# A decayed linear attention and two gated layers on one core: the norm without small instructions, the own term of the first tiles summed by TensorE, and r multiplied as it leaves PSUM

## The chip, the core and the metric

The kernel runs on one core of a Trainium2 chip. The core has five engines with their own instruction queues: TensorE (PE in the profile; its weight loads are listed apart as PEld), VectorE (DVE), ScalarE (ACT), GpSimd (POOL) and SyncE (SP), which here only issues DMA transfers. Matmuls write PSUM, eight banks of 128 partitions by 512 float32. The metric is the time of one execution on the device in microseconds; of several runs the median.

## The reference, cut to what matters

Three things follow each other. First an attention with a decaying state over 4 batches, 8 heads, 768 steps and head size 48:

```python
for t in range(S):
    kt, vt, rt = k[:, :, t], v[:, :, t], r[:, :, t]
    cur = np.einsum('bhd,bhe->bhde', u[None] * kt, vt)
    y[:, :, t] = np.einsum('bhd,bhde->bhe', rt, state + cur)
    state = w[None, :, :, None] * state + np.einsum('bhd,bhe->bhde', kt, vt)
```

Its output, as 3072 tokens of 384 columns, is normalised and goes through two gated layers of width 1536:

```python
rms = np.sqrt(np.mean(x * x, axis=-1, keepdims=True) + 1e-06)
xn = x / rms * rms_g
g = xn @ w_gate                       # layer one: silu(g) * (xn @ w_val) @ w_out
...
gate = 1.0 / (1.0 + np.exp(-(x @ w_gate)))
return (gate * (x @ w_val) @ w_out).astype(np.float32)   # layer two
```

The term with u is what a token contributes to its own output: for each head the sum over d of r, u and k, times v. It is called the own term below. The weights of the two layers come as float64 and are turned into float32 on the chip.

## The kernel before

**Tiles and blocks.** The tokens are cut into 24 tiles of 128 (tile i is chunk i // 4 of batch i % 4, so tiles 0 to 3 are the first chunk of each batch and start without a state), and into 6 blocks of four tiles for the gated layers. A layer takes each block through 12 steps, one for every 128 columns of the width of 1536; a step multiplies x with a piece of w_gate and a piece of w_val (lines 687 to 689: three float32r products each, of the high and low parts of weights and x) and accumulates the product with a piece of w_out (line 714). Layer one's six blocks are followed by layer two's. The 36 pieces of layer one's weights are fetched and converted in the first block's steps (ScalarE lines 66, 71 and 649, VectorE lines 80, 81 and 652, GpSimd line 87).

**A tile of attention** (`attention(i)`, from line 459) works with k divided and r multiplied by powers of w, taken from the middle of the tile. VectorE or GpSimd makes kq = kn * wk and rq = rn * wr (line 474); for tiles 1 to 7 TensorE turns both (line 332) and ScalarE moves them from PSUM into kT and rT (line 498); from tile 8 on the turn goes through DRAM. Tile 0's k and r are turned raw in the set-up and multiplied with the powers tq and tp, which lie in the buffers o[2] and o[1], as they leave PSUM (line 322). TensorE then computes scores and state change (`both`, lines 508 and 513) into two banks; VectorE masks the scores into aa (line 519), and forms zh, the state in the middle of the tile (a copy, line 527, in tiles 0 to 3; a sum with z, line 529, later), and zu (line 532). The result (lines 541 and 548) needs zh and aa, and VectorE adds the own term vc while it takes the result out of PSUM into x (line 554).

**The own term** vc is made by two products, a reduction to cf and a product with vn (lines 474, 483, 474).

**The norm:** ScalarE squares x with a running sum (line 563), VectorE folds a check on that sum into ok (line 565) and turns the sum into the mean plus epsilon (line 568), GpSimd raises it to the power -1/2 (line 473), and VectorE scales x by it and by g (line 572). TensorE turns x (line 583), and ScalarE and VectorE make xh and xl from it (lines 587 and 589), which the steps read.

**Order.** Nothing is ordered by hand. Every instruction, or small group, is added to a plan with a duration estimate per engine, a due time, and the tokens it reads and writes; `Plan.run` then simulates the engines with these estimates and emits each engine's instructions in the order that comes out. A task that names two engines ("VG") goes to the one that the plan finds done first. A changed estimate, or a task less, can therefore change the order of the whole beginning. On the chip each engine runs its list in order and waits where it must.

Of the kernel before, what the change touches and what calls it, by code (L numbers as in the profile page):

```python
# [15 lines left out]
P = 128  # L16
# [214 lines left out]
def blocked(  # L231
# [36 lines left out]
    wsafe = const.tile([HS, NPAIR], F32, name="wsafe")  # L268
    p2 = const.tile([HS, 8, NPAIR], F32, name="p2")
# [9 lines left out]
    totals = const.tile([P, 2 * 3 * NF], F32, name="totals")  # L279
    mhalf = const.tile([P, 1], F32, name="mhalf")  # L280
# [40 lines left out]
    def mul(e, out, x, y, op=ALU.mult):  # L321
        e.tensor_tensor(out=out, in0=x, in1=y, op=op)
# [11 lines left out]
    def setup():  # L334
# [130 lines left out]
    def attention(i):  # L465
# [16 lines left out]
        add("VG", (0.47, 1.02), d + 1, either(vc[i2], vc[i2], u_bc, ALU.mult), (), [("vc", i2)])  # L482
        add("V", 0.46, d + 3, lambda: nc.vector.tensor_reduce(
            out=cf[i2].rearrange("p h o -> p (h o)"), in_=vc[i2], axis=AX.X, op=ALU.add), [("vc", i2)], [("cf", i2)])
        add("VG", (0.47, 0.9), d + 4, either(vc[i2], vn[i3], cf[i2].to_broadcast([P, H, D]), ALU.mult),
            [("v", i3), ("cf", i2)], [("vc", i2)])
# [71 lines left out]
        if not last:  # L558
# [3 lines left out]
        t = ss[i2]  # L562
# [403 lines left out]
```

## Time and profile before

| | us |
|---|---|
| median of 3 runs (1031.54 to 1032.87) | 1032.0 |
| the profiled execution | 1029.34 |
| its span, first to last instruction | 1027.7 |
| TensorE busy in the span | 1002.4 (98%) |
| VectorE | 490.4 (48%) |
| ScalarE | 341.7 (33%) |
| GpSimd | 140.2 (14%) |

The profile is of one execution. Busy times are of the whole span; the kernel has stretches with different limits, so a share of the whole says little about any one of them. TensorE's clock as granted was 0.989 of full in the mean; it is at half in parts of the first 50 us.

### The profile page before, as it was taken

To read this page: it belongs to the slowest core of one execution; us is meant where nothing else is said; L and a number is where in the kernel's file an instruction comes from. 1 tells how busy PE (TensorE), PEld (TensorE's weight loads), DVE (VectorE), ACT (ScalarE), POOL (GpSimd) and SP (SyncE) were. 2 spreads that over 40 slices of the span, in tenths; PEclk is the share of its full clock that TensorE was granted. 3 is DMA by queue.
4 is the path that set the end of the run, shared out by engine and by line. 5 is a ranking of instruction groups with operands and counts; after the bars stand their busy time and mean duration, and the time that the engine had idled before them with its cause. 6 is when DMAs were issued, how large, how long until landed. Compare 5 with 4: busy or idle time off the path is not lost.

```text
span 1027.7 us, 19397 instructions
## 1 busy us (share of the span) xinstructions
PE 1002.4 (98%) x7938; PEld 831.1 (81%) x7938; DVE 490.4 (48%) x993; ACT 341.7 (33%) x710; POOL 140.2 (14%) x170
## 2 busy tenths in 40 slices
PE   7799999999999999999999999999999999999997
PEld 6577777787787777778888888888888888888886
DVE  7889995645655664653555322222222223222222
ACT  3577552223333333334555312222212222112221
POOL 4443432212321320211110000000000000000000
PEclk8899999999999999999999999999999999999998
DMA  8916356555884785653654100100100000000001
GB/s 195 274 41 157 91 110 143 106 104 129 178 175 123 156 189 135 145 148 94 198 171 147 62 1 3 59 1 22 40 1 31 32 1 5 27 1 27 4 1 34
DMA packets 213761, 91.40 MB, mean 89 GB/s; under 512 B 156576, under 2 KB 205984, under 8 KB 213664
## 3 DMA queue, kind: packets, MB, share of 16 engines
q1 hardware_dynamic: 213664, 90.08, 35.3%
q8 instruction: 64, 1.05, 0.5%
q14 instruction: 33, 0.27, 0.1%
HBM read 64.10 MB, written 25.95 MB: 88 GB/s over the span
## 4 chain that ended last, share of the span: by engine, by line
PE 87%; DVE 8%; DMA 1%; ACT 1%; issue 1%; POOL 0%; SPq 0%; DVEq 0%; POOLq 0%; ACTq 0%
PE bank L714 27%; PE bank L687 18%; PE bank L688 18%; PE bank L689 18%; PE bank L548 2%; DVE wraw L81 1%; PE bank L541 1%; PE bank L508 1%; DVE w L652 1%; DVE wt L80 1%; DVE hl L699 1%; DMA rn<-in_r_dram 1%; PE bank L513 1%; DVE vc L474 1%; DVE sg L696 0%
## 5 line engine op out<-in xcount | busy, mean ns | idle before, releaser
L687 PE MATMUL bank<-xh,w 128*128 128x512 f32 x864 | 344.5, 399 | 1.8 <-ACT w L649 1.1
L689 PE MATMUL bank<-xh,w 128*128 128x512 f32 x864 | 342.5, 396 | 0.3 <-DVE w L652 0.3
L688 PE MATMUL bank<-xl,w 128*128 128x512 f32 x864 | 342.6, 397 | 0.0
L696 DVE TENSOR_TENSOR sg<-bank,sg 128x512 f32<-128x512 f32 x144 | 99.2, 689 | 371.5 <-PE bank L689 368.2
L689 PEld LDWEIGHTS bank<-xh,w 128*128 128x128 f32 x864 | 162.7, 188 | 40.7 <-DVE w L652 2.3
L687 PEld LDWEIGHTS bank<-xh,w 128*128 128x128 f32 x864 | 162.8, 188 | 39.2 <-ACT w L649 2.4
L688 PEld LDWEIGHTS bank<-xl,w 128*128 128x128 f32 x864 | 162.8, 188 | 35.4 <-DVE xl L589 0.3
L694 ACT ACTIVATE sg<-bank 128x512 f32<-128x512 f32 x144 | 85.9, 597 | 294.0 <-PE bank L689 293.9
L698 ACT ACTIVATE hh<-sg 128x512 fp32r<-128x512 f32 x144 | 90.7, 630 | 238.5 <-DVE sg L696 238.5
L714 PE MATMUL bank<-w,hh 128*128 128x384 f32 x576 | 158.7, 337 | 0.0
L714 PE MATMUL bank<-hh,w 128*128 128x512 f32 x432 | 151.3, 401 | 0.7 <-DVE w L652 0.7
L699 DVE TENSOR_TENSOR hl<-sg,hh 128x512 fp32r<-128x512 f32 x144 | 102.2, 710 | 65.3 <-ACT hh L698 65.0
L714 PEld LDWEIGHTS bank<-w,hh 128*128 128x128 f32 x576 | 105.0, 188 | 3.4
L714 PEld LDWEIGHTS bank<-hh,w 128*128 128x128 f32 x432 | 81.0, 188 | 21.2 <-DVE w L652 1.6
L714 PE MATMUL bank<-w,hl 128*128 128x384 f32 x288 | 96.7, 336 | 0.0
L714 PE MATMUL bank<-hl,w 128*128 128x512 f32 x216 | 85.4, 395 | 0.0
L87 POOL TENSOR_TENSOR wt<-wraw 128x384 int32<-128x384 int32 x36 | 33.1, 918 | 200.1 <-DVE wraw L81 118.8
L66 ACT ACTIVATE wt<-wraw 128x384 f32<-128x384 f32 x72 | 39.7, 552 | 51.5 <-DMA wraw<-in_moe_w_gate_dram 23.0
L714 PEld LDWEIGHTS bank<-w,hl 128*128 128x128 f32 x288 | 54.1, 188 | 3.3 <-DVE hl L699 0.3
L714 PEld LDWEIGHTS bank<-hl,w 128*128 128x128 f32 x216 | 40.6, 188 | 8.7
L87 POOL TENSOR_TENSOR wraw<-wraw 128x384 int32<-128x384 int32 x36 | 37.8, 1060 | 54.4 <-DVE wraw L81 31.4
L81 DVE SCALAR_TENSOR_TENSOR wraw<-wraw,wt 128x384 int32<-128x384 int32 x72 | 41.8, 589 | 1.4
(122 smaller groups left out, 712.6 us busy)
## 6 DMA issues: line engine op xcount, KB each, us to landing
wraw<-in_moe_w_gate_dram SPq DMA_DIRECT2D x24, 384.0 KB, 4.4
wraw<-in_moe_w_val_dram SPq DMA_DIRECT2D x24, 384.0 KB, 4.5
wraw<-in_moe_w_out_dram SPq DMA_DIRECT2D x24, 384.0 KB, 5.0
parked<-wt SPq DMA_DIRECT2D x36, 192.0 KB, 2.7
wt<-parked SPq DMA_DIRECT2D x36, 192.0 KB, 2.4
kn<-in_k_dram SPq DMA_DIRECT2D x24, 192.0 KB, 3.7
rn<-in_r_dram SPq DMA_DIRECT2D x24, 192.0 KB, 4.1
vn<-in_v_dram SPq DMA_DIRECT2D x24, 192.0 KB, 3.8
```

The costliest lines, as they stand in the source:

```text
L66: nc.scalar.activation(t.bitcast(F32), raw[:, :, 1].bitcast(F32), AF.Abs, scale=2.0 ** -112, accum_out=total)
L81: yield nc.vector.scalar_tensor_tensor(out=high, in0=high, scalar=-(1 << 31), in1=t, op0=ALU.bitwise_and, op1=ALU.bitwise_or)
L87: nc.gpsimd.tensor_tensor(out=out, in0=raw[:, :, 1], in1=raw[:, :, 0], op=ALU.add)
L548: nc.tensor.matmul(yp[n][part(s)][ts, p * D:(p + 1) * D], aa[0][part(s), n, p, ts], vn[i3][part(s), 2 * p + n, :], start=(first and not s ...
L687: nc.tensor.matmul(ps, whi[f][:, kind, ws], xh[b2][:, c, :], start=(c == 0), stop=False)
L688: nc.tensor.matmul(ps, whi[f][:, kind, ws], xl[b2][:, c, :], start=False, stop=False)
L689: nc.tensor.matmul(ps, wlo[f][:, kind, ws], xh[b2][:, c, :], start=False, stop=(c == KC - 1))
L694: add("A", 0.6, d - STEP, lambda g: nc.scalar.activation(sg[n2], g, gate), [("g", n)], [("sg", n2)], psum=[("g", n)])
L696: add("V", 0.69, d + 1 - STEP, lambda ps: nc.vector.tensor_tensor(out=sg[n2], in0=ps, in1=sg[n2], op=ALU.mult), [("value", n)], [("sg", n2 ...
L698: add("A", 0.63, d + 1 - STEP, lambda: nc.scalar.activation(hh[n2], sg[n2], AF.Copy), [("sg", n2)], [("hh", n2)])
L699: add("VG", (0.69, 1.5), d + 1 - STEP, lambda e: by[e].tensor_tensor(out=hl[n2], in0=sg[n2], in1=hh[n2].bitcast(F32), op=ALU.subtract), [( ...
L714: nc.tensor.matmul(a[:, :rhs.shape[-1]], lhsT, rhs, start=(f == 0 and i == 0), stop=(f == NF - 1 and i == 2))
```

## The change

Three edits. In the **norm**, x and vc become views of buffers that are one column wider (x_ and vc_); that column of x_ holds the square root of EPS * 384, so the scaled sum of squares over 385 columns is the mean plus epsilon at once. The steps at lines 565 and 568 are gone; the sums of all tiles stay in `squares` and are checked with three instructions in `weights_ok`, late in layer one. GpSimd's power reads the sum itself.

For tiles 0 to 3 the **own term** is made otherwise: VectorE multiplies kT by rT (in which the powers of w cancel but for one factor w), TensorE multiplies that product with uw = u * w, one column per pair of heads and half tile, into the last four columns of the two banks of scores, and VectorE multiplies vn with these columns as they leave PSUM, a half tile at a time. uw is loaded by two more transfers in the set-up.

In tiles 1 to 7 **r** is turned raw, and VectorE multiplies it with the powers while it moves it from PSUM into rT; the product rq on VectorE or GpSimd and ScalarE's move are gone. In tiles 0 to 3 ScalarE, not VectorE, copies zh.

```diff
+    uw = const.tile([HS, NPAIR], F32, name="uw")
+    squares = const.tile([P, NTILE], F32, name="squares")
...
+    x_, vc_ = ring("x", 2, [P, DM + 1]), ring("vc", 2, [P, DM + 1])
+    x, vc = [t[:, :DM] for t in x_], [t[:, :DM].rearrange("p (h d) -> p h d", h=H) for t in vc_]
...
         load_heads(kn[0], k, 0, 0)
         load_heads(rn[0], r, 0, 0)
+        for n in range(2):
+            nc.sync.dma_start(out=uw[rows(n)], in_=u.rearrange("(p a) d -> a d p", a=2)[n])
...
+        for t in x_:
+            nc.gpsimd.memset(t[:, DM:], (EPS * DM) ** 0.5)
...
+    def own_factors():
+        mul(nc.vector, uw, uw, wsafe)
...
-        if i:
+        if by_dma:
             add("VG", (0.47, 1.02), d - 2, either(rq_, rn_, heads(wr), ALU.mult), [("r", i2)], ["rq"])
-        add("VG", (0.47, 1.02), d + 1, either(vc[i2], rn_, kn_, ALU.mult), [("r", i2), ("k", i2)], [("vc", i2)])
...
+        by_sums = i < B
+        if not by_sums:
+            add("VG", (0.47, 1.02), d + 1, either(vc[i2], rn_, kn_, ALU.mult), [("r", i2), ("k", i2)], [("vc", i2)])
...
-            for nm, src, read, dst in (("kT", kq[i2], ("kq", i2), kT[i2]), ("rT", rq[0], "rq", rT[i2])):
+            for nm, src, read, dst in (("kT", kq[i2], ("kq", i2), kT[i2]), ("rT", rn[i2], ("r", i2), rT[i2])):
...
-                add("A", 0.48, d + (nm == "rT"), lambda ps, dst=dst: nc.scalar.activation(dst[:HS], pairs(ps), AF.Copy),
-                    [name(nm)], tokens, psum=[name(nm)])
+                if nm == "kT":
+                    add("A", 0.48, d, lambda ps, dst=dst: nc.scalar.activation(dst[:HS], pairs(ps), AF.Copy),
+                        [name(nm)], tokens, psum=[name(nm)])
+                else:
+                    add("V", 0.6, d + 1, lambda ps, dst=dst: nc.vector.tensor_tensor(out=dst[:HS], in0=pairs(ps), in1=pairs(o[1]), op=ALU.mult),
+                        [name(nm), ("o", 1)], tokens, psum=[name(nm)])
...
+        if by_sums:
+            prod, token = ((o[0], ("o", 0)), (sg[0], ("sg", 0)))[i2]
+            add("V", 0.6, d + 3, lambda: nc.vector.tensor_tensor(out=pairs(prod), in0=kT[i2], in1=rT[i2][:HS], op=ALU.mult),
+                [(t, i2, n) for t in ("kT", "rT") for n in range(2)], [token], port=True)
+            own = lambda sp: sp[:, N - NPAIR:]
+
+            def sums(*sp):
+                for p in range(NPAIR):
+                    for s in range(2):
+                        for n in range(2):
+                            nc.tensor.matmul(own(sp[n])[part(s), p:p + 1], pairs(prod)[rows(n), p, part(s)], uw[rows(n), p:p + 1],
+                                             start=True, stop=True)
+            add("T", 0.5, d + 4, sums, [token, "uw", name("sp")], [name("own")], psum=banks)
+            for n in range(2):
+                add("V", 0.27, d + 5, lambda sp, n=n: nc.vector.tensor_tensor(
+                    out=half_of(vc[i2], n), in0=half_of(vn[i3], n), in1=own(sp).unsqueeze(2).to_broadcast([P, NPAIR, D]), op=ALU.mult),
+                    [name("own"), ("v", i3)], [("vc", i2)], psum=[banks[n]])
...
-            add("V", 0.27, d + 4, lambda sp: nc.vector.tensor_copy(zh[i2], u3(sp)), [name("sp")], [("zh", i2)], psum=banks[:1])
+            add("A", 0.27, d + 4, lambda sp: nc.scalar.activation(zh[i2], u3(sp), AF.Copy), [name("sp")], [("zh", i2)], psum=banks[:1])
...
-        add("A", 0.5, d + 7, lambda: nc.scalar.activation(flat(vc[i2]), x[i2], AF.Square, accum_out=t[:, 0:1]),
-            [("x", i2)], [("vc", i2), ("ss", i2)])
-        add("V", 0.07, d + 20, lambda: nc.vector.scalar_tensor_tensor(
-            out=ok, in0=t[:, 0:1], scalar=3e38, in1=ok, op0=ALU.is_le, op1=ALU.mult), [("ss", i2)], ["ok"])
-        t_ = small[i2]
-        add("V", 0.07, d + 8, lambda: nc.vector.tensor_scalar(
-            out=t_[:, 0:1], in0=t[:, 0:1], scalar1=1.0 / DM, scalar2=EPS, op0=ALU.mult, op1=ALU.add),
-            [("ss", i2)], [("rms", i2)])
-        add("G", 0.55, d + 8, tt(nc.gpsimd, t_[:, 1:2], t_[:, 0:1], mhalf, ALU.pow), (), [("rms", i2)])
+        mean, t_ = squares[:, i:i + 1], small[i2]
+        add("A", 0.5, d + 7, lambda: nc.scalar.activation(vc_[i2], x_[i2], AF.Square, scale=DM ** -0.5, accum_out=mean),
+            [("x", i2)], [("vc", i2), ("square", i)])
+        add("G", 0.55, d + 8, tt(nc.gpsimd, t_, mean, mhalf, ALU.pow), [("square", i)], [("rms", i2)])
...
+        nc.vector.tensor_scalar(out=squares, in0=squares, scalar1=3e38 / DM, scalar2=None, op0=ALU.is_le)
+        nc.vector.tensor_reduce(out=one, in_=squares, axis=AX.X, op=ALU.min)
+        mul(nc.vector, ok, ok, one)
...
+    plan.add("V", 0.1, DUE[0][0], own_factors, (), ["uw"])
```

The plan puts out another order. On VectorE, the list right after the set-up's last product (into rT of tile 0) before; the number behind a name marks one buffer, so that rT_115 is tile 0's and rn_96 and kn_98 are tile 1's:

```order
L322 TENSOR_TENSOR rT_115<-bank_76,o_139 112x512
L474 TENSOR_TENSOR vc_105<-rn_95,kn_97 128x384
L474 TENSOR_TENSOR kq_103<-kn_98,wk 128x8x48
L474 TENSOR_TENSOR vc_105<-vc_105,u_bc 128x384
L474 TENSOR_TENSOR rq_104<-rn_96,wr 128x8x48
L483 TENSOR_REDUCE cf_107<-vc_105 128x8
L519 TENSOR_TENSOR aa_117<-bank_73,mask 128x4x64
L519 TENSOR_TENSOR aa_117<-bank_74,mask 128x4x64
L474 TENSOR_TENSOR vc_105<-vn_99,cf_107 128x384
L527 COPY zh_124<-bank_73 112x192
```

and now, with o_139 the powers for r and o_138 the product of kT and rT of tile 0:

```order
L327 TENSOR_TENSOR rT_113<-bank_76,o_139 112x512
L327 TENSOR_TENSOR uw<-uw,wsafe 112x4
L547 TENSOR_TENSOR o_138<-kT_111,rT_113 112x512
L487 TENSOR_TENSOR kq_105<-kn_100,wk 128x8x48
L519 TENSOR_TENSOR rT_114<-bank_73,o_139 112x512
L327 TENSOR_TENSOR sg_133<-sg_133 112x4 x3
L327 TENSOR_TENSOR p_84<-sg_133 112x4
L438 COPY wc<-p_84 112x192
L540 TENSOR_TENSOR aa_115<-bank_74,mask 128x4x64
L540 TENSOR_TENSOR aa_115<-bank_75,mask 128x4x64
L559 TENSOR_TENSOR vc_118<-vn_101,bank_74 128x4x48
L571 TENSOR_TENSOR zu_126<-bank_75,zh_124 112x192
```

The two products into vc, the reduction and the copy of zh are gone from between set-up and tile 0's own part; uw, the product of kT and rT, and tile 1's rT stand there, and the state factors wc have moved ahead of aa.

On TensorE, the instructions at the start of the first step (xh_128 with w), before; vn_100 is tile 4's v, and x_119 tile 3's x:

```order
L548 MATMUL bank_78<-vn_100,aa_117 32x48 x4
L548 MATMUL bank_77<-vn_100,aa_117 32x48 x4
L583 MATMUL bank_75<-ident,x_119 128x128 x3
L687 MATMUL bank_73<-xh_128,w_803 128x512
L688 MATMUL bank_73<-xl_130,w_803 128x512
L689 MATMUL bank_73<-xh_128,w_803 128x512
```

and now, where vn_101 is tile 3's v, rn_97 tile 4's r, x_116 tile 2's x and x_117 tile 3's:

```order
L587 MATMUL bank_73<-vn_101,aa_115 32x48 x4
L587 MATMUL bank_79<-vn_101,aa_115 32x48 x4
L337 MATMUL bank_80<-ident,rn_97 112x128 x4
L616 MATMUL bank_76<-ident,x_116 128x128 x3
L616 MATMUL bank_77<-ident,x_117 128x128 x3
L720 MATMUL bank_74<-xh_128,w_804 128x512
L721 MATMUL bank_74<-xl_130,w_804 128x512
```

The scores and the result of tile 4 stood ahead of the first step; now only the turn of its r does, with the turns of x of tiles 2 and 3.

On ScalarE, around the first two xh (line 587), before:

```order
L587 ACTIVATE xh_128<-bank_79 128x3x128
L563 ACTIVATE vc_106,ss_110<-x_119 128x384
L66 ACTIVATE wt_146,totals<-wraw_313 128x384
L71 ACTIVATE wraw_313<-wraw_313 128x384
L498 ACTIVATE kT_114<-bank_75 112x512
L498 ACTIVATE rT_116<-bank_73 112x512
L587 ACTIVATE xh_128<-bank_74 128x3x128
```

and now, where L620 is the step into xh and L566 the copy zh of tiles 2 and 3:

```order
L602 ACTIVATE vc_119,squares<-x_117 128x385
L620 ACTIVATE xh_128<-bank_73 128x3x128
L566 ACTIVATE zh_124<-bank_78 112x192
L66 ACTIVATE wt_146,totals<-wraw_320 128x384
L71 ACTIVATE wraw_320<-wraw_320 128x384
L620 ACTIVATE xh_128<-bank_77 128x3x128
L566 ACTIVATE zh_125<-bank_75 112x192
L602 ACTIVATE vc_118,squares<-x_116 128x385
```

Each of the two copies zh stands right behind a step into xh that belongs to the tile two before it.

## Rows read from the trace of the kernel before

**Rows 1.** Stretches: busy us of PE, PEld, DVE, ACT, POOL; granted clock; DMA share, GB/s:
```profile
11.20:46.10 34.90, 25.13 (x780) 20.70 (x780) 29.79 (x82) 15.71 (x41) 14.96 (x15) 0.80 1.01 253
46.10:141.00 94.90, 90.38 (x828) 69.02 (x829) 90.26 (x181) 64.91 (x164) 40.02 (x40) 0.98 0.43 112
141.00:1028.00 887.00, 879.02 (x6291) 734.10 (x6290) 363.43 (x685) 257.56 (x496) 80.68 (x91) 1.00 0.32 79
12.00:18.00 6.00, 4.85 (x110) 4.13 (x105) 5.60 (x16) 2.58 (x7) 2.80 (x2) 0.50 1.14 278
```

**Rows 2.** TensorE's waits, longest first, 11.2 to 46.1: total us, times, longest:
```profile
PE bank L541 <- DVE zh L527: 2.6, 2, 1.4
...
```

**Rows 3.** TensorE's longest wait, 46.1 to 141 us:
```profile
PE bank L687 <- ACT w L649: 1.1, 2, 0.8
```

**Rows 4.** VectorE's groups, 11.2 to 141 us: busy us, mean ns | idle before, releaser:
```profile
...
L699 DVE TENSOR_TENSOR hl<-sg,hh 128x512 fp32r<-128x512 f32 x11 | 8.8, 799 | 1.0 <-ACT hh L698 0.9
...
L554 DVE TENSOR_TENSOR x<-bank,vc 128x192 f32<-128x192 f32 x16 | 5.5, 348 | 1.7 <-PE bank L548 1.6
L474 DVE TENSOR_TENSOR vc<-rn,kn 128x384 f32<-128x384 f32 x8 | 5.0, 625 | 0.0
L474 DVE TENSOR_TENSOR vc<-vc,u_bc 128x384 f32<-128x384 f32 x8 | 4.4, 547 | 0.0
L483 DVE TENSOR_REDUCE cf<-vc 128x8 f32<-128x384 f32 x8 | 4.3, 540 | 0.0
L474 DVE TENSOR_TENSOR vc<-vn,cf 128x384 f32<-128x384 f32 x6 | 4.3, 712 | 0.0
L565 DVE SCALAR_TENSOR_TENSOR ok<-ss,ok 128x1 f32<-128x1 f32 x8 | 3.9, 494 | 0.0
L474 DVE TENSOR_TENSOR rq<-rn,wr 128x384 f32<-128x384 f32 x6 | 3.9, 648 | 0.1
L589 DVE TENSOR_TENSOR xl<-bank,xh 128x384 fp32r<-128x384 f32 x7 | 3.9, 554 | 2.4 <-ACT xh L587 2.4
L474 DVE TENSOR_TENSOR kq<-kn,wk 128x384 f32<-128x384 f32 x6 | 3.3, 549 | 0.7 <-DMA kn<-in_k_dram 0.7
...
L474 DVE TENSOR_TENSOR z<-zu,wc 112x192 f32<-112x192 f32 x5 | 1.7, 346 | 0.0
L527 DVE COPY zh<-bank 112x192 f32<-112x192 f32 x4 | 1.4, 348 | 0.0
...
L568 DVE TENSOR_SCALAR rms<-ss 128x1 f32<-128x1 f32 x8 | 1.2, 145 | 0.0
L322 DVE TENSOR_TENSOR rT<-bank,o 112x512 f32<-112x512 f32 x1 | 0.7, 681 | 0.0
```

**Rows 5.** Timeline 36.2 to 38.5 us: start, duration, engine, instruction:
```profile
36.28 0.15 DVE L565 SCALAR_TENSOR_TENSOR ok<-ss,ok 128x1 f32<-128x1 f32 x1
36.35 0.35 DVE L80 TENSOR_SCALAR wt<-wt 128x384 int32<-128x384 int32 x1
...
37.59 0.83 POOL L87 TENSOR_TENSOR wraw<-wraw 128x384 int32<-128x384 int32 x1 [3.63 <-DVE rms L568]
...
37.75 0.68 DVE L565 SCALAR_TENSOR_TENSOR ok<-ss,ok 128x1 f32<-128x1 f32 x1
```

**Rows 6.** TensorE's timeline, tile five (from 88 us) and tile zero (13.57):
```profile
13.57 0.89 PE L513 MATMUL bank<-vn,kq 64*48 64x48 f32 x32 [1.15 <-POOL kq L474]
...
88.50 0.60 PE L332 MATMUL bank<-ident,kq 128*112 128x128 f32 x4
...
92.33 0.71 PE L508 MATMUL bank<-rT,kT 48*64 48x64 f32 x32 [0.69 <-ACT rT L498]
92.84 0.55 PE L513 MATMUL bank<-vn,kq 64*48 64x48 f32 x32
...
98.37 0.32 PE L541 MATMUL bank<-z,rT 48*64 48x48 f32 x4
...
99.12 0.89 PE L548 MATMUL bank<-vn,aa 64*32 64x48 f32 x64
```

More of the change, by code (lines that the diff above doesn't have):

```diff
@@ L279, in blocked @@
     totals = const.tile([P, 2 * 3 * NF], F32, name="totals")
+    squares = const.tile([P, NTILE], F32, name="squares")
     mhalf = const.tile([P, 1], F32, name="mhalf")
     rn, kn, vn = ring("rn", 2, [P, H, PAD]), ring("kn", 2, [P, H, PAD]), ring("vn", 3, [P, H, D])
-    kq, rq, vc = ring("kq", 2, [P, H, PAD]), ring("rq", 1, [P, H, PAD]), ring("vc", 2, [P, H, D])
-    cf, ss, small = ring("cf", 2, [P, H, 1]), ring("ss", 2, [P, 1]), ring("rms", 2, [P, 2])
+    kq, rq = ring("kq", 2, [P, H, PAD]), ring("rq", 1, [P, H, PAD])
+    cf, small = ring("cf", 2, [P, H, 1]), ring("rms", 2, [P, 1])
     kT, rT, aa = ring("kT", 2, [HS, NPAIR, P]), ring("rT", 2, [P, NPAIR, P]), ring("aa", 1, [P, 2, NPAIR, P])
-    x, z = ring("x", 2, [P, DM]), ring("z", B, [HS, NPAIR, D])
+    x_, vc_ = ring("x", 2, [P, DM + 1]), ring("vc", 2, [P, DM + 1])
+    x, vc = [t[:, :DM] for t in x_], [t[:, :DM].rearrange("p (h d) -> p h d", h=H) for t in vc_]
+    z = ring("z", B, [HS, NPAIR, D])
     zh, zu = ring("zh", 2, [HS, NPAIR, D]), ring("zu", 2, [HS, NPAIR, D])
@@ L347, in setup @@
             nc.sync.dma_start(out=wT[rows(n)], in_=w.rearrange("(p a) d -> a d p", a=2)[n])
-        for t in (kn[0], rn[0], kq[1], rq[0]):
+        nc.gpsimd.memset(uw, 1.0)
+        for t in (kn[0], rn[0], kq[1], rn[1], rq[0]):
             nc.gpsimd.memset(t[:, :, D:], 0.0)
@@ L477, in attention @@
         add("VG", (0.47, 1.02), d - 2, either(kq_, kn_, heads(wk), ALU.mult), [("k", i2)], [("kq", i2)])
-        if i:
+        if by_dma:
             add("VG", (0.47, 1.02), d - 2, either(rq_, rn_, heads(wr), ALU.mult), [("r", i2)], ["rq"])
-        add("VG", (0.47, 1.02), d + 1, either(vc[i2], rn_, kn_, ALU.mult), [("r", i2), ("k", i2)], [("vc", i2)])
[L482 to L486, printed above, removed]
+        by_sums = i < B
+        if not by_sums:
+            add("VG", (0.47, 1.02), d + 1, either(vc[i2], rn_, kn_, ALU.mult), [("r", i2), ("k", i2)], [("vc", i2)])
+            add("VG", (0.47, 1.02), d + 1, either(vc[i2], vc[i2], u_bc, ALU.mult), (), [("vc", i2)])
+            add("V", 0.46, d + 3, lambda: nc.vector.tensor_reduce(
+                out=cf[i2].rearrange("p h o -> p (h o)"), in_=vc[i2], axis=AX.X, op=ALU.add), [("vc", i2)], [("cf", i2)])
+            add("VG", (0.47, 0.9), d + 4, either(vc[i2], vn[i3], cf[i2].to_broadcast([P, H, D]), ALU.mult),
+                [("v", i3), ("cf", i2)], [("vc", i2)])
         if by_dma:
@@ L559, in attention @@
             add("VG", (0.27, 0.6), d + 10, either(z[b], zu[i2], wc, ALU.mult), ["wc", ("zu", i2)], [("z", b)])
-        t = ss[i2]
-        add("A", 0.5, d + 7, lambda: nc.scalar.activation(flat(vc[i2]), x[i2], AF.Square, accum_out=t[:, 0:1]),
-            [("x", i2)], [("vc", i2), ("ss", i2)])
-        add("V", 0.07, d + 20, lambda: nc.vector.scalar_tensor_tensor(
-            out=ok, in0=t[:, 0:1], scalar=3e38, in1=ok, op0=ALU.is_le, op1=ALU.mult), [("ss", i2)], ["ok"])
-        t_ = small[i2]
-        add("V", 0.07, d + 8, lambda: nc.vector.tensor_scalar(
-            out=t_[:, 0:1], in0=t[:, 0:1], scalar1=1.0 / DM, scalar2=EPS, op0=ALU.mult, op1=ALU.add),
-            [("ss", i2)], [("rms", i2)])
-        add("G", 0.55, d + 8, tt(nc.gpsimd, t_[:, 1:2], t_[:, 0:1], mhalf, ALU.pow), (), [("rms", i2)])
+        mean, t_ = squares[:, i:i + 1], small[i2]
+        add("A", 0.5, d + 7, lambda: nc.scalar.activation(vc_[i2], x_[i2], AF.Square, scale=DM ** -0.5, accum_out=mean),
+            [("x", i2)], [("vc", i2), ("square", i)])
+        add("G", 0.55, d + 8, tt(nc.gpsimd, t_, mean, mhalf, ALU.pow), [("square", i)], [("rms", i2)])
         add("V", 0.53, d + 9, lambda: nc.vector.scalar_tensor_tensor(
-            out=x[i2], in0=x[i2], scalar=t_[:, 1:2], in1=g_bc, op0=ALU.mult, op1=ALU.mult), [("rms", i2)], [("x", i2)], port=True)
+            out=x[i2], in0=x[i2], scalar=t_, in1=g_bc, op0=ALU.mult, op1=ALU.mult), [("rms", i2)], [("x", i2)], port=True)
         to = (slice(None), slice(None), slice(col * P, (col + 1) * P))
@@ L793, in blocked @@
         if (bi, f) == (turn - 1, NF - 1):
-            plan.add("V", 0.6, at[turn, 3], weights_ok, [("total", i) for i in range(2 * 3 * NF)], ["ok"])
+            plan.add("V", 0.6, at[turn, 3], weights_ok, [("total", i) for i in range(2 * 3 * NF)] + [("square", i) for i in range(NTILE)], ["ok"])
             plan.add("T", 0.1, at[turn, 3], count_bad, ["ok"], ["count"], psum=["count"])
```

## The prediction

> **What bounds the kernel now.** I read the table of stretches first, cut where the work changes character: the set-up of the powers of w (to 11.2 us), the first four tiles of attention (to 46.1, where TensorE begins the first GLU step), the stretch until tile seven's x stands ready in xh and xl (141.0), and the rest [rows 1]. In the rest TensorE is busy 879.0 of 887.0 us, and the list of waits names none for TensorE there; the 8 us that are left are the tail behind its last matmul. Nothing on another engine can shorten that stretch. All that can be won lies in the first 141 us.
>
> In 11.2 to 46.1 TensorE is busy 25.1 of 34.9 us and VectorE 29.8; in 46.1 to 141.0 both are busy 90.3 or 90.4 of 94.9, so neither has room [rows 1]. TensorE's longest wait in the first of the two is for zh, a copy on VectorE, 2.6 us in two waits; in the second the longest are for a piece of weights, 1.1 us in two [rows 3]. I take VectorE as the bound of both stretches: it runs its list almost without a gap, and TensorE's gaps end when VectorE gets to the next item. The DMA share of 1.01 in the first stretch [rows 1] is the other candidate; against it speaks that VectorE waited for a transfer only 0.7 us there, for kn [rows 4], because most of the traffic is weights fetched far ahead.
>
> **The change, part by part.** I count VectorE's instructions in the order of both kernels from the end of set-up to the eighth subtraction into xl (tile seven's). Both have the same 35 pieces of weights and the same GLU instructions in between, so the stretches compare, and the mean durations of the stretch 11.2 to 141 price the rest [rows 4].
>
> What goes, 41 instructions: 8 of ok at 0.494 us (3.95), 8 of rms at 0.145 (1.16), 4 reductions into cf at 0.540 (2.16), 5 products into rq at 0.648 (3.24; six were there and one, tile eight's, stays), of the products into vc 3 of rn by kn at 0.625 (1.88), 4 by u_bc at 0.547 (2.19) and 2 of vn by cf at 0.712 (1.42), 3 of z at 0.346 that the planner now gives to GpSimd (1.04), and 4 copies zh at 0.348 that go to ScalarE (1.39). Sum 18.4 us.
>
> What comes, 22 instructions: 7 products of a transposed r in PSUM with the powers, 112x512, for which the set-up's own rT is the same instruction, 0.681 (4.77); 4 products of kT by rT, 112x512 out of SBUF, which the trace does not have: between 0.549 (kq, 384 wide) and 0.799 (hl, 512 wide), and I take 0.681 (2.72); 8 half-width products of vn with the own term out of PSUM, like the sums into x, 0.348 (2.78); 2 more of kq, which GpSimd had, 0.549 (1.10); one product uw, 0.15. Sum 11.5 us.
>
> The difference is 6.9 us of durations. Neighbours overlap: an ok lasts 0.15 us and the next instruction begins 0.07 behind it [rows 5], so each of the 19 fewer instructions gives 0.08 less, 1.5 in all. VectorE's list is **5.4 us** shorter.
>
> Not all of this need arrive. An ok lasts 0.15 us alone, and 0.68 where GpSimd's product had begun 0.16 us earlier [rows 5]; the mean of 0.494 holds 0.34 of such waiting, 8 x 0.34 = 2.7 us. If the next instruction inherits the wait, only 2.7 us are left. Against that, GpSimd itself loses 2 products rq, 3 vc and at least one kq, about 1 us each, and takes 3 z, so there is less to collide with. I keep nearly all of it.
>
> ScalarE loses seven evictions into rT and takes four copies zh; it is busy 15.7 of 34.9 and 64.9 of 94.9 us [rows 1], so its load costs nothing, its order may (below). With the rms step one hop goes out of each tile's norm, and GpSimd's power now follows ScalarE's sum directly; that is hidden except ahead of the first GLU step. Later tiles lose ok and rms too, where VectorE is busy 363 of 887 us [rows 1]: nothing. The three instructions on squares near the end of layer one run beside full TensorE: nothing; uncovered they would be some 0.5 us. SP issues two small loads for uw behind the first r, ahead of u, g and the first v; the first gap on a load, 0.7 us for kn, bounds what they can add in one place, and I put them at nothing.
>
> TensorE gets 64 matmuls, 16 for each of four tiles, with the shape of stationary operand that scores and state have. A group of 16 costs 0.55 us (state) or 0.71 (scores) for tile five, and 0.89 (state) for tile zero [rows 6], where the granted clock is 0.50, the lower of its two levels [rows 1]; no row has a moving operand one column wide, so 0.55 to 0.89 each, **2.2 to 3.6 us** in all; less than nothing it can't be, as it is added work. They fall in the stretch where TensorE is idle 9.8 us [rows 1].
>
> Where does it show? The 4.5 us that TensorE idles in the second stretch are the second cover to look at. The planner now begins the first GLU step ahead of tile four's scores and results; it used to run them first. From tile five's rows, scores and state take 1.1 us, the result 1.6, the turn of kq 0.5 (a row of 0.60, less the overlap): 3.2 us [rows 6] move behind the start. VectorE has 65 instructions up to the last xl ahead of that start, where it had 82; by the same prices 24.0 us instead of 29.8, and with the idle time left as it was, 34.9 - 29.8 = 5.1, the GLU starts at 11.2 + 24.0 + 5.1 = 40.3 us, 5.8 earlier. Behind it VectorE has as much as before (0.1 less by the same count), TensorE 90.4 + 3.2 = 93.6 in 94.9. That is tight; I let 0.4 to 1.0 us of it come back as waiting. 5.8 less that agrees with 5.4 less a little, and I take **5.0 us**.
>
> One rule of the Trainium skill speaks against the fourth idea of the change, multiplying r out of PSUM. The rows first: 128x384 out of PSUM into xl takes 0.554 us, 128x384 out of SBUF by u_bc 0.547 [rows 4]. "VectorE: DVE Perf Modes", in "The TRN2 errata — SBUF-src ops pay a fixed extra latency per instruction", lists 120 cycles plus the columns out of PSUM against 58 out of SBUF; as an estimate from that page, 62 cycles at 0.96 GHz on 15 new instructions would be 1.0 us and the gain 4.0. The rows show 7 ns, so the sum goes by the rows.
>
> **The rivals.** *The wait is handed on.* VectorE's two-input and small instructions stand still while GpSimd works; take one out and the next stands still. Then VectorE saves 2.7, and tile four's work behind the start gives 1.0 back: 1.7 us, 1030.3. For it: the four oks of the second stretch sit between pieces of weights that need the same access. Against: GpSimd's shorter list. The page "SBUF — State Buffer" ("SBUF: two separate sides") says the pair of ports that VectorE and GpSimd share is an exclusive lock and that the loser blocks for the whole instruction; the two ok rows agree [rows 5].
>
> *ScalarE becomes the chain.* zh of tile two now stands in ScalarE's queue behind the xh of tile zero, which waits for TensorE to turn x, which waits for VectorE's norm; TensorE's result of tile two waits for zh. Queued behind the waiting xh are zh, the next square and the weights' conversions. Each of tiles two and three can lose up to what TensorE's gap for zh has been, 1.4 us at most [rows 2], and in ScalarE's queue some two or three times that, 3 to 4 us each. It decides once the GLU starts later than 46.1 - 3.2 = 43 us, since 3.2 us of TensorE's work are now behind the start. At 45 us the kernel is 2 us slower: 1034.
>
> *More than VectorE's list.* TensorE's waits for zh (2.6 us) go with the copy, and the idle 5.1 us of VectorE shrink as the chain shortens. Then the start comes at 37 to 38 and some 3 us more are won: 8 us, 1024.
>
> That the change does not do what it says is excluded by the order: the instructions named are gone.
>
> **How the numbers follow.** The profiled execution took 1029.34 us, of which 1027.7 is its span; the timed runs have a median of 1032.0, 2.7 above it, and I take the difference over. 1029.3 - 5.0 = 1024.3 for a profiled execution, **1027.0** for the median. Forecast: chance 0.55, gain 3 to 7 us (1025 to 1029). Handed on: 0.20, 1029 to 1032. More: 0.15, 1022 to 1025. ScalarE's chain: 0.10, 1032 to 1035. The range 1022 to 1031.5 leaves out the last and the edges. A measurement of this kernel tells 0.2%, 2.1 us, from no change: faster than 1029.9 are the first and third, 0.71 with an edge of the second; within, most of the second and an edge of the last, 0.19; slower 0.10.
>
> **What would show it.** Right: the first GLU matmul at 39 to 42 us; VectorE about 24 us busy from set-up to there; no row of ok or rms; rT from PSUM at 0.68 us and the sums at 0.55 to 0.9 us a tile; still no wait of TensorE after some 136 us, with its busy time there unchanged. The handed-on wait would show as a longer mean of the weights' bit operations and of the norm's scaling. ScalarE's chain would show as a wait of TensorE's result for zh from ScalarE of over 1.5 us, and a start after 43. The forecast falls if the start is early but TensorE's idle time from there to tile seven's x grows past 4.5 us: then the pieces of weights, and not the tiles, set the pace.

## The result: 12 us less, from where the buffers lie

The changed kernel takes 1019.67 us (median of 4 runs, 1018.02 to 1020.59) where the kernel before, run beside it, takes 1031.77: ratio 0.9886, 95% interval 0.9867 to 0.9904. The forecast was 1027.0, range 1022.0 to 1031.5; the time lies under it and the gain is more than twice the one I worked out. The profiled spans are 1017.9 and 1027.7 us.

The same stretches as in [rows 1], of the changed kernel (the last ends with the shorter span; columns as there):

```profile
11.20:46.10 34.90, 24.47 (x741) 21.22 (x741) 21.83 (x62) 12.51 (x35) 6.16 (x9) 0.71 1.02 241
46.10:141.00 94.90, 90.37 (x986) 71.54 (x987) 89.90 (x178) 65.27 (x163) 42.12 (x42) 0.96 0.43 117
141.00:1018.00 877.00, 867.90 (x6300) 736.61 (x6298) 363.37 (x661) 257.26 (x500) 78.95 (x89) 1.00 0.32 80
```

VectorE lost its work as planned: it is 24.0 us busy from set-up to the first GLU matmul in place of 29.8 (the row stands below, with the prediction). But that matmul (L720, before L687) begins at 48.27 us, 2.2 later than before. The gain is in the last row, in the stretch that I had called fixed: 877 us in place of 887. TensorE's rows there say how. Two windows of 60 us in which it does GLU matmuls alone, in layer one and in layer two, of the kernel before and then of the changed one:

```profile
490.00:550.00 60.00, 60.00 (x259) 48.33 (x258) 34.27 (x67) 33.15 (x71) 7.14 (x8) 1.00 0.59 185
700.00:760.00 60.00, 60.00 (x290) 52.40 (x289) 16.05 (x24) 14.48 (x24) 0.00 (x0) 1.00 0.08 27
```

```profile
490.00:550.00 60.00, 60.00 (x267) 49.67 (x266) 35.89 (x70) 32.43 (x70) 7.19 (x8) 1.00 0.57 176
700.00:760.00 60.00, 60.00 (x292) 52.97 (x291) 16.45 (x24) 14.17 (x23) 0.00 (x0) 1.00 0.08 27
```

TensorE is busy all 60 us at full clock in all four, yet it does 267 matmuls where it did 259. From the starts in the trace, 512-column matmuls in a row follow each other every 233.3 ns before (mostly 231 and 236; the mean of 1,556 spacings in layer one's steps 12 to 72). After the change it is 226.7 ns once a row has settled (227.3 over as many). A step of layer one takes 6.12 us in place of 6.30, one of layer two 6.23 in place of 6.28. **A share of busy time hides this**: an engine at 100% may still have two speeds.

The starts of the GLU steps split the time (the first matmul of step 0, and the lengths to step 12, to step 72 where layer two begins, and to step 143; us):

| kernel | step 0 | 0 to 12 | 12 to 72 | 72 to 143 |
|---|---|---|---|---|
| before | 46.11 | 95.64 | 423.40 | 446.22 |
| changed | 48.27 | 95.17 | 415.54 | 442.22 |
| before_moved | 44.97 | 96.65 | 414.42 | 442.22 |
| before_layout | 46.24 | 97.08 | 414.87 | 442.23 |
| after_3 | 50.94 | 95.09 | 416.28 | 442.23 |
| before_layout_slow | 44.04 | 94.65 | 423.04 | 446.22 |
| after_moved_3 | 45.76 | 95.30 | 426.74 | 446.22 |

(The last five are experiments.) Steps 0 to 12 gain next to nothing; I put that down to VectorE, which is as busy as TensorE there. The speed gives 7.9 us in steps 12 to 72 and 4.0 in layer two; the start takes 2.2 back.

What differs for those matmuls? Not their order or shapes. The change makes x and vc one column wider, adds uw and squares and drops ss. In the built program each buffer takes a multiple of 32 bytes a partition, so all that is declared later moves. The weights lie at 352 modulo 512 bytes before and at 480 after; xh, xl, hh and hl at 32 before and at 224 after. The distance from xh to the weights is 320, or 64 modulo 128, before, and 256, or 0 modulo 128, after.

### The profile page after: what moved, and what is told of

Its sections match the earlier page's. It is cut to its first block, busy times and chain, and to the rows that moved or that the text cites. A ratio compares the mean times of both kernels' runs of the same rounds, so it can differ in the third digit from the quotient of the medians.

```text
span 1017.9 us, 19601 instructions
## 1 busy us (share of the span) xinstructions
PE 990.9 (97%) x8066; PEld 836.9 (82%) x8066; DVE 482.0 (47%) x947; ACT 338.6 (33%) x707; POOL 132.0 (13%) x168
## 4 chain that ended last, share of the span: by engine, by line
PE 85%; DVE 6%; DMA 3%; issue 3%; ACT 2%; SPq 1%; POOL 0%; DVEq 0%; POOLq 0%; ACTq 0%
PE bank L747 27%; PE bank L720 18%; PE bank L722 17%; PE bank L721 17%; PE bank L587 2%; PE bank L529 1%; DVE wraw L81 1%; PE bank L580 1%; DVE w L685 1%; PE bank L534 1%; DMA wraw<-in_moe_w_out_dram 1%; DVE wt L80 1%; DMA turn_x<-vc 1%; DMA rn<-in_r_dram 1%; PE bank L337 1%
## 5 line engine op out<-in xcount | busy, mean ns | idle before, releaser
L720 PE MATMUL bank<-xh,w 128*128 128x512 f32 x864 | 340.0, 394 | 0.6 <-ACT xh L620 0.6
L722 PE MATMUL bank<-xh,w 128*128 128x512 f32 x864 | 338.8, 392 | 0.8 <-DVE w L685 0.8
L721 PE MATMUL bank<-xl,w 128*128 128x512 f32 x864 | 338.6, 392 | 0.0
L720 PEld LDWEIGHTS bank<-xh,w 128*128 128x128 f32 x864 | 162.7, 188 | 34.1 <-ACT xh L620 1.0
L747 PE MATMUL bank<-hh,w 128*128 128x512 f32 x432 | 148.8, 396 | 0.0
```

The source lines that it names most:

```text
L720: nc.tensor.matmul(ps, whi[f][:, kind, ws], xh[b2][:, c, :], start=(c == 0), stop=False)
L721: nc.tensor.matmul(ps, whi[f][:, kind, ws], xl[b2][:, c, :], start=False, stop=False)
L722: nc.tensor.matmul(ps, wlo[f][:, kind, ws], xh[b2][:, c, :], start=False, stop=(c == KC - 1))
L747: nc.tensor.matmul(a[:, :rhs.shape[-1]], lhsT, rhs, start=(f == 0 and i == 0), stop=(f == NF - 1 and i == 2))
```

## Experiments

**Before's program on the changed kernel's addresses, and the reverse.** Two theories: *addresses* set the spacing, or the *stream* of TensorE's instructions does. A buffer that nothing uses moves all that is declared behind it (the names of the buffers are left out).

```
 before_moved (kernel before):         before_32:
+    const.tile([P, 32], F32, ...)     +    const.tile([P, 8], F32, ...)
+    work.tile([P, 16], F32, ...)
 after_moved (changed kernel):         after_32:
+    const.tile([P, 224], F32, ...)    +    const.tile([P, 8], F32, ...)
+    work.tile([P, 240], F32, ...)
```

> The kernel before with none of the change: two unused buffers (128 and 64 bytes a partition) put its weights, xh, xl, hh and hl on the byte addresses that they have in the changed kernel; the order of instructions is that of before on every engine. In the trace of before, 512-column matmuls follow each other every 233.3 ns (231 and 236 in turn, 2,747 of 2,817 spacings at 229 ns or more); in the changed kernel every 226.7 ns (2,119 of 2,827 at 228 ns or less). Theory 'addresses' (where the operands lie sets the spacing): 226.7 ns here too, 10 to 15 us less in layer one and 4 in layer two, 1032 - 12 to 18 = 1014 to 1020 us. Rival 'stream' (what the change does to TensorE's instruction stream sets it, or what it took from VectorE): 233.3 ns and 1029 to 1033 us.

> The changed kernel whole, with two unused buffers (896 and 960 bytes) that put weights, xh, xl, hh and hl on the addresses of the kernel before modulo 512 bytes (weights at 352, the others at 32). 'Addresses': spacing 233.3 ns, and what the change is worth by itself shows: the start of the first layer was 2.2 us later in the changed kernel and the steps up to the end of attention took about 2 us more beside the spacing, so 1032 + 2 to 5 = 1034 to 1037 us. 'Stream': 226.7 ns and 1018 to 1021 us as in the changed kernel.

> The kernel before, all weights and working buffers 32 bytes further: weights at 0 modulo 128 bytes, xh, xl, hh and hl at 64 (before: 96 and 32). 'Addresses' in the form 'a row is read in pieces of 64 bytes, and one that begins in the middle of a piece costs one more': 512 columns are 32 whole pieces, spacing 220 ns or less, 1032 - 3,240 x 0.0133 - 864 x 0.007 = 983 us. In the form 'the distance between weights and moving rows modulo 128 counts' (64 as in before, 0 in the changed kernel): 233.3 ns, 1032 us. 'Stream': 233.3 ns, 1029 to 1033 us.

> The changed kernel, all weights and working buffers 32 bytes further: weights, xh, xl, hh and hl at 0 modulo 128 bytes (changed kernel: all at 96). 'Pieces of 64 bytes': 220 ns or less for 512 columns, 1019.7 - 3,240 x 0.0067 - 864 x 0.007 = 992 us. 'Distance': 226.7 ns, 1018 to 1021 us. 'Stream': 226.7 ns, 1018 to 1021 us.

before_moved: 1014.56 us, ratio 0.9833 [0.9803, 0.9864]; after_moved: 1027.94, 0.9968 [0.9951, 0.9985]; before_32: 1030.13; after_32: 1017.29. The window in layer one of before_moved and of after_moved:

```profile
490.00:550.00 60.00, 60.00 (x267) 49.67 (x266) 35.87 (x69) 33.89 (x72) 7.20 (x8) 1.00 0.58 184
```

```profile
490.00:550.00 60.00, 60.00 (x259) 48.35 (x258) 34.03 (x68) 33.42 (x71) 6.29 (x7) 1.00 0.58 180
```

*Addresses* holds, in both directions: with none of the change TensorE does 267 matmuls, with all of it 259. The theory of pieces of 64 bytes falls: with every operand on a multiple of 64 the spacing is 233.3 (before_32) and 226.7 ns (after_32), as the distance says. I had expected after_moved at 1034 to 1037; that it came under the kernel before left open what the change itself is worth.

**Other distances.** The kernel before with 320, 32 or 96 bytes ahead of the working buffers (`work.tile([P, 80], F32, ...)`, with 8 or 24 in place of 80), so that only xh, xl, hh and hl move against the weights.

> The kernel before with an unused buffer of 320 bytes ahead of the working buffers: weights and xh, xl, hh, hl all at 352 modulo 512 bytes. Distance from xh to the weights, modulo 512: 0 here, 256 in the fast kernels so far (changed kernel, before_moved, after_32), 320 in the slow ones. Theory 'distance modulo 128': 0 as in the fast ones, 226.7 ns a 512-column matmul and about 1014.5 us. Rival 'distance modulo 256 or 512, two reads that meet in the same part of the buffer': 0 is the worst case and 233.3 ns or more, 1031 us or more.

> The kernel before with an unused buffer of 32 bytes ahead of the working buffers: weights stay at 352 modulo 512, xh, xl, hh and hl move to 64; distance 288 modulo 512, 32 modulo 128. 'Distance': a third value that nothing so far shows, between 220 ns (1005 us) and 240 ns (1045 us); if the spacing falls step by step with the distance from the slow 64 to the fast 0 modulo 128, 230 ns and 1023 us. A rule on the weights' own address alone (352 in all slow kernels so far but before_32) has nothing to move: 233.3 ns, 1031 us.

> The kernel before with an unused buffer of 96 bytes ahead of the working buffers: weights at 352 modulo 512, xh, xl, hh and hl at 128; distance 224 modulo 512, 96 modulo 128. 'Distance': the fourth value modulo 128; by the step-by-step form 230 ns and 1023 us, by 'only 0 is fast' 233.3 ns and 1031 us.

The window in layer one at distance 0, then at 288:

```profile
490.00:550.00 60.00, 60.00 (x267) 49.67 (x266) 36.14 (x69) 34.80 (x73) 7.65 (x8) 1.00 0.60 185
```

```profile
490.00:550.00 60.00, 60.00 (x259) 48.31 (x258) 35.88 (x67) 33.86 (x72) 6.14 (x7) 1.00 0.59 184
```

Steps of layer one take 6.12 us at distance 0, 6.30 at 288 and 6.30 at 224; the times are 1017.74 (2 runs), 1035.20 (1.0036 [1.0023, 1.0049]) and 1030.84. So of the four distances modulo 128 **only 0 is fast**, wherever the pair lies (96 and 96, or 0 and 0), and whether it is 0 or 256 modulo 512; that two equal addresses modulo 512 would meet and be the worst case falls. The weights' own address, the same in all three, is not what counts. The slow distances differ a little in layer two: 6.313 us a step at 288, 6.287 at 224, 6.280 before.

**Only the output matmuls' operands moved.** before_moved, with 32 bytes between sg and hh.

```
+    work.tile([P, 8], F32, ...)     # between sg and hh
```

> before_moved with 32 bytes between sg and hh: xh and xl stay at 96 modulo 128 with the weights, hh and hl go to 0. If each matmul's spacing follows the operands that TensorE reads at that time, the 18 matmuls of a step that stream xh or xl keep 226.7 ns and the 9 of layer one that stream hh or hl go to 233.3: 6.18 us a step in layer one in place of 6.12, 4.3 us more in all, about 1019 us; in layer two, where the weights stream and hh and hl are loaded, the 12 output matmuls change. If one unequal operand slows the whole stream, 6.30 us a step and 1030 us; if it is xh and xl alone that count, 6.12 us and 1014 to 1016 us.

In layer one the 9 matmuls that stream hh and hl come every 233 ns, and the 18 that stream xh and xl come back from there to 226.7 within about eight: 6.22 us a step. So it is decided by what TensorE reads at that time, with an after-effect on the next few matmuls, which my 6.18 had left out. In layer two, where weights stream and hh and hl are loaded, the 384-column matmuls take 174.0 ns in place of 175.5 and a step 6.213 us, the least of all runs. Its 2 runs are too few for a verdict on the time (1014.47 and 1020.38).

**What is the change worth without the addresses?** First the change without the sums, then repeats, then one layout for both.

```
 after_no_sums (changed kernel):
-        by_sums = i < B
+        by_sums = False
...                           # the memset, the loads and the product of uw go too
```

> The changed kernel, addresses as it has them, but tile 0 to 3's own term is made by VectorE and GpSimd as in the kernel before (no loads of uw, no product, no sums on TensorE; VectorE gets back the groups vc, cf). In the changed kernel TensorE stood still for 3.7 and 2.1 us ahead of the first layer with no releaser in the trace, at its 1,466th and 954th instruction; before_moved, without the change, stood for 1.0 us at its 957th. Theory 'supply': TensorE runs out of instructions there, and the 256 that the sums add (32 matmuls and 32 weight loads a tile) bring it to each such point earlier than the next instructions come; without them the start comes 2 to 3 us earlier than in the changed kernel (48.3 and 46.5 in two profiles), at 44 to 45, and the time is 1014 to 1016 us. Rival 'VectorE': the sums saved VectorE four calls a tile, so putting them back costs 1 to 3 us: 1019 to 1022 us, start at 48 to 49.

1021.44 us (1018.93 to 1025.01), start at 47.86: no gain, so *supply* alone does not explain the late start; the numbers are those of the rival. VectorE has its work back: it is busy 30.4 us from set-up to the start (11.2 to 47.86 us). TensorE's waits in this run from 11 to 48 us:

```profile
PE bank L526 <- ACT vc L599: 2.1, 1, 2.1
PE bank L337 <- DMA rn<-in_r_dram: 2.0, 2, 1.5
PE bank L613 <- DVE x L602: 1.4, 1, 1.4
PE bank L577 <- ACT zh L563: 1.1, 1, 1.1
PE bank L584 <- issue: 0.8, 1, 0.8
```

The waits without a releaser shrink to 0.8 us, and others stand in their place.

> before_moved once more (the kernel before, its operands on the addresses of the changed kernel), beside the changed kernel in the same group of runs. The question is what the change is worth with addresses out of it. Theory 'nothing at the start': 1014 to 1018 us, 1 to 3 us under the changed kernel. Rival 'my forecast of 5 us less for the change itself': 1018 to 1021 us, above the changed kernel.

> The changed kernel once more, beside before_moved_2. 'Nothing at the start': 1017 to 1020 us, no lower than before_moved_2, and the first layer starts at 45 to 48.5 us, within the 45.0 to 46.9 us of the five profiles of the kernel before's instruction order or later. 'My forecast': 5 us under before_moved_2, at 1010 to 1014 us, start at 40 to 41 us.

> after_moved once more (the changed kernel on addresses of the kernel before modulo 512), beside the kernel before itself. It gave 0.9968 [0.9951, 0.9985] of its time. If the change is worth about 3 us there, 0.996 to 0.998 again; if that was scatter, 0.999 to 1.002.

Medians 1018.25, 1020.23 and 1028.15 us (0.9972 [0.9955, 0.9990]). before_moved_2 is 3.7 us above before_moved, the same program, and their ranges do not meet (up to 1015.77, from 1016.13). Of the 3.5 us between the two profiled spans, 1.3 lie ahead of the GLU, 1.0 in steps 0 to 72 and 1.2 behind the start of step 143. So a difference of 3 us between two groups of runs shows nothing by itself. Still, the change seemed worth 3 us less on one set of addresses and 2 us more on the other. The last four runs, one group, take out what still differed: buffers in the changed kernel's order and widths in both.

```
 before_layout (kernel before; before_layout_slow adds the two buffers of after_moved):
+    const.tile([HS, NPAIR], F32, name="uw")
...
+    const.tile([P, NTILE], F32, name="squares")
...
-    x, z = ring("x", 2, [P, DM]), ring("z", B, [HS, NPAIR, D])
+    x_, vc_ = ring("x", 2, [P, DM + 1]), ring("vc", 2, [P, DM + 1])
+    x, vc = [t[:, :DM] for t in x_], [t[:, :DM].rearrange("p (h d) -> p h d", h=H) for t in vc_]
...
+    ss = ring("ss", 2, [P, 1])   # declared last
```

> The kernel before with every shared buffer on the byte address that it has in the changed kernel (buffers declared in the changed kernel's order and width, uw and squares there but unused); its order of instructions is that of before. Beside after_3. Theory 'the change is worth nothing at the start, the rest is layout': within 1.5 us of after_3, at 1018 to 1021 us, and 2 to 3 us above before_moved. Rival 'the change costs 2 to 3 us where the matmuls run at 226.7 ns, since TensorE then bounds the start': 2 to 3 us under after_3, at 1016 to 1018 us. Rival 'my forecast': 5 us above after_3.

> The changed kernel once more, for the same group of runs as before_layout: 1018 to 1021 us by every theory.

> The kernel before with every shared buffer on the byte address that it has in after_moved (spacing 233.3 ns by all theories). 'The rest is layout': within 1.5 us of after_moved_3, 1026.5 to 1030 us. 'The change is worth 3 us there': 3 us above after_moved_3, 1030 to 1033 us. 'My forecast': 5 us above.

> after_moved once more, for the same group of runs as before_layout_slow: 1027 to 1029 us by every theory.

before_layout 1019.64 us (6 runs) against after_3 1020.99: ratios to the kernel before 0.9894 [0.9879, 0.9910] and 0.9894 [0.9875, 0.9913]. before_layout_slow 1029.59 (11 runs) against after_moved_3 1028.48: 0.9982 [0.9970, 0.9994] and 0.9974 [0.9963, 0.9985]. **On one layout the change is worth nothing that can be measured**: the time is 1.4 us longer on the fast one and 1.1 shorter on the slow one. From the scatter of these runs I estimate that the means differ by between -2.1 and +3.5 us on the fast layout and -1.8 and +0.8 on the slow one (95%); a gain of 2 us or less could hide there, the 5.0 of my forecast could not. The layout alone takes the kernel before from 1031.1 to 1019.6 us, 11.5 less, where the whole change, in the same group of runs, takes 10.1.

## Where the change's own gain went

The kernel before's instruction order began the GLU at 42.6 to 46.9 us in its ten profiles (mean 45.6), the changed kernel's at 45.3 to 50.9 in seven (47.1). TensorE's waits from 8 to 50 us in the changed kernel (waiting line, releaser, which is what ended the wait, or "issue" where the trace names nothing: us, times, longest):

```profile
PE bank L587 <- issue: 3.7, 1, 3.7
PE bank L616 <- DVE x L605: 2.4, 1, 2.4
PE bank L616 <- issue: 2.1, 1, 2.1
PE bank L337 <- DMA rn<-in_r_dram: 1.8, 1, 1.8
```

Where [rows 2] had 2.6 us for zh, 0.5 are left; these four are new. The sharpest count is over VectorE's whole list, from 11.2 us to the eighth subtraction into xl, by the trace: 242 instructions and 113.3 us busy in the changed kernel, 261 and 120.2 before. The list is 6.9 us shorter, but VectorE's idle time in it grew from 10.2 to 19.0 us, nearly all of that ahead of the first GLU matmul, and its end came at 143.5 us in place of 141.6. The other profiles agree: 7.3 to 12.2 us idle in the old order, 17.0 to 22.0 in the changed one.

Where TensorE stands still, in order of time, in after_3 (start, length, matmuls, in brackets the idle time ahead):

```profile
32.34 0.80 PE L616 MATMUL bank<-ident,x 128*128 128x128 f32 x3 [4.72 <-issue]
...
41.24 0.56 PE L587 MATMUL bank<-vn,aa 64*32 64x48 f32 x22
44.18 1.11 PE L587 MATMUL bank<-vn,aa 64*32 64x48 f32 x42 [2.39 <-issue]
45.23 1.10 PE L337 MATMUL bank<-ident,rn 128*112 128x128 f32 x4
46.13 0.85 PE L616 MATMUL bank<-ident,x 128*128 128x128 f32 x3
49.40 0.90 PE L616 MATMUL bank<-ident,x 128*128 128x128 f32 x3 [2.43 <-DVE x L605]
```

and in before_layout:

```profile
29.84 0.71 PE L553 MATMUL bank<-vn,aa 64*32 64x48 f32 x47
31.96 0.40 PE L553 MATMUL bank<-vn,aa 64*32 64x48 f32 x17 [1.41 <-issue]
```

TensorE stops in the middle of a group of equal matmuls, 22 of 64 done, where nothing can be waited for but the next instruction. Count what it has done at each stop. The changed kernel to 28.1 and 37.85 us, then after_3 to 27.7 and 41.8:

```profile
0.00:28.10 28.10, 23.38 (x476) 21.13 (x477) 18.30 (x81) 10.19 (x28) 7.85 (x32) 0.76 0.91 189
0.00:37.85 37.85, 29.81 (x732) 26.45 (x733) 24.81 (x99) 14.42 (x41) 10.37 (x36) 0.82 0.92 202
```

```profile
0.00:27.70 27.70, 21.51 (x476) 19.17 (x477) 18.27 (x82) 10.27 (x28) 7.82 (x32) 0.82 0.90 193
0.00:41.80 41.80, 30.46 (x732) 26.58 (x733) 24.90 (x98) 14.35 (x41) 10.33 (x36) 0.80 0.95 215
```

953 and 1,465 matmuls and weight loads in both, and 956 in before_layout, at another place of the program (to 30.5 us, 478 of each). These two stops come 512 instructions apart; smaller ones stand at the 443rd (in three of the changed order's profiles, 1.9 to 2.2 us) and, in after_3, at the 699th (0.8 us). The changed kernel's page lists a queue with 65 packets of instructions, 16,384 bytes each by the trace (queue, packets, MB, share of the DMA engines):

```profile
q8 instruction: 65, 1.06, 0.5%
```

I take it for TensorE's, because each of these stops ends 2.3 to 3.0 us after one of its packets begins. In "Runtime: NRT & Kernel Launch", "Instruction fetch mechanics", the Trainium skill says that instructions come in blocks of 16 KiB, 256 of them, and that the cost of crossing a block is mostly hidden. The sizes agree, since the stops are one or two such blocks apart, but by this reading the crossings are not hidden here. With the DMA share at 0.9 to 1.0, TensorE's waits without a releaser make 2.7 to 7.9 us in all ahead of the GLU in the changed order (mean 5.0 of seven profiles, 11 to 52 us) and 0.5 to 1.5 in the old one (mean 1.0 of ten). That the busy DMA queues delay the packets was not tried.

The other two: ahead of the start TensorE now turns tile three's x with nothing to do meanwhile (2.4 us for L605), because tile four's scores and results, which filled that time, moved behind it. And the turn of tile one's raw r, which now stands ahead of the first scores, waits 1.8 to 2.1 us for its load in three of the seven profiles.

This account is read from the waits; the one run that took a stop away, after_no_sums, put other waits in its place. What each of them costs by itself was not tried.

Part of the scatter in the old order goes with the clock. In 20 to 55 us, outputs_32, then before_moved, one and the same order of instructions:

```profile
20.00:55.00 35.00, 26.72 (x611) 20.87 (x610) 33.13 (x81) 21.75 (x56) 18.11 (x19) 1.00 0.87 256
```

```profile
20.00:55.00 35.00, 28.46 (x643) 23.06 (x636) 30.71 (x77) 19.04 (x49) 14.52 (x17) 0.80 0.89 256
```

At a granted clock of 1.00 throughout (2.4 GHz) the GLU began at 42.6 us, at a mean of 0.80 (part of it at 1.2 GHz) at 45.0. From 11.2 to 42.6 us the granted clock is 0.63 to 0.95 in the ten profiles of the old order (mean 0.78) and 0.62 to 0.77 in the seven of the changed one (0.71). How much of the later start is the clock was not separated.

## The prediction, point by point

**"Nothing on another engine can shorten that stretch": the step that failed.** It is true as worded, but I drew from it that the stretch was fixed. TensorE's own rate was a term of the sum that I never wrote down, and it gave 7.9 us in steps 12 to 72 and 4.0 in layer two: more than the 9.8 by which the spans differ. No row of before shows that another layout is faster; the only hint was that the change widened buffers ahead of the GLU's operands.

That the kernel became faster, as I forecast, is luck: the gain came from where its buffers happened to fall, not from the list that I added up.

**VectorE's list: right.** Up to the first GLU matmul I counted 65 instructions and 24.0 us:

```profile
11.20:48.27 37.07, 25.37 (x745) 21.73 (x745) 24.00 (x65) 13.59 (x39) 7.19 (x10) 0.70 1.02 244
```

The prices held too (us and mean ns of one; the stretch 11.2 to 141):

```profile
L605 DVE SCALAR_TENSOR_TENSOR x<-x,rms,g_bc 128x384 f32<-128x384 f32 x8 | 5.4, 680 | 0.0
L519 DVE TENSOR_TENSOR rT<-bank,o 112x512 f32<-112x512 f32 x7 | 4.8, 682 | 0.7 <-PE bank L337 0.7
L559 DVE TENSOR_TENSOR vc<-vn,bank 128x192 f32<-128x192 f32 x8 | 2.8, 344 | 0.0
L547 DVE TENSOR_TENSOR o<-kT,rT 112x512 f32<-112x512 f32 x2 | 1.4, 681 | 0.0
L327 DVE TENSOR_TENSOR uw<-uw,wsafe 112x4 f32<-112x4 f32 x1 | 1.0, 966 | 0.0
```

rT out of PSUM 0.682 (0.681 said), the product of kT and rT 0.681, the half-width products 0.344 (0.348). Only uw, beside a product of GpSimd's, took 0.97 in place of 0.15. Over the whole list the 5.4 us that I worked out were 6.9.

**"The idle time left as it was, 5.1": failed.** VectorE is idle 37.07 - 24.00 = 13.1 us up to the start. I had taken VectorE for the bound of the stretch and its idle time for a constant. With 5.8 us off its list, TensorE's waits for instructions, for the last x and for rn end last, and VectorE waits with it. 11.2 + 24.0 + 5.1 gave 40.3; the measured starts are 45.3 to 50.9. Of the 5.0 us of gain nothing can be measured on one layout (1.4 us longer and 1.1 shorter).

**Tile four's work moved behind the start** I booked as 3.2 us won there. It had been cover: without it the 2.4 us of x show.

**The sums at 0.55 to 0.89 us a tile.** Nearly right as a duration (0.60 to 1.03 in after_3; at the 1.03 the granted clock is 0.50). But I priced them by their matmul time alone: with their weight loads they are 64 instructions a tile, 256 in all, one packet more, and they move the places where TensorE stops. That this costs time in the end is not shown, since after_no_sums is no faster.

**The loads of uw at nothing:** nothing speaks against it. TensorE waits up to 2.1 us for rn, but after_no_sums, which does not load uw, has that wait too (1.5 us, 2.0 in two): it comes with the raw r turned so early, which I had not looked at.

**The rivals.** ScalarE's chain falls: the start is past 43 us, its condition, but TensorE waits 0.5 us for zh, not over 1.5. The wait handed on falls as I had described it: its sign, longer bit operations and a longer scaling in the norm, is absent. The two bit operations took 473 and 612 ns (478 and 624 before), and the scaling 680 ns (L605 above), where it took 908 before:

```profile
L572 DVE SCALAR_TENSOR_TENSOR x<-x,rms,g_bc 128x384 f32<-128x384 f32 x8 | 7.3, 908 | 0.4 <-POOL rms L473 0.4
```

The gain was lost in another way: as VectorE's idle time, in waits of TensorE. "More than VectorE's list" gave 1024, and the time lies lower still, for another reason.

## To carry to other kernels

Before crediting a change with time in a stretch that it does not touch, look at the spacing of equal matmuls there, and put the old program on the new addresses: a few unused bytes are a cheap control. Here 512-column fp32r matmuls run 3% faster when streamed rows and weights lie a multiple of 128 bytes apart, and the kernel before with 192 unused bytes (1014.56 and 1018.25 us) is as good as the whole change or better. And an engine that is busy 85% of a stretch bounds it only as far as the next list is shorter; add up the second engine's list, with its instructions and not only its time.

## What the runs showed of the hardware

- 512-column fp32r matmuls in layer one, each with its weight load: 226.7 ns apart, once settled, where the streamed rows and the weights have equal byte addresses modulo 128, and 233.3 where they lie 32, 64 or 96 apart. In the Trainium skill, "SBUF — State Buffer" ("A bandwidth-pool intuition that's wrong (but worth ruling out)") gives weight loads a second, independent read port; by that, the distance should not matter, and the runs say it does. Why, no run here shows.
- In layer two the 384-column matmuls go the other way: 175.5 ns in the fast layouts, 173.9 before, 174.0 with only hh and hl off. The difference is in the first six spacings of a row of 12 (177.6 against 173.5 ns); the others are 173.4 and 173.8. At a distance of 32 the mean is 176.9.
- TensorE stood still where nothing but its next instruction was missing: in the seven profiles of the changed order 1.6 to 4.7 us at the 954th (five times; twice the trace names VectorE's aa there, 1.3 and 1.5) and 0.8 to 3.7 at the 1,466th (six times), the latter inside a group of equal matmuls.
